# A delta-rule attention block and its SwiGLU block on one core: the third chunk moved to the seven-product scheme

## The chip, the cores and the metric

The kernel runs on one core of a Trainium2 chip. The metric is the device time in microseconds (us) of one execution, as the median of several runs. A core has five engines that each work through their own list of instructions in order: TensorE (PE, with its weight loads PEld) multiplies matrices into PSUM, VectorE (DVE) and ScalarE (ACT) do elementwise work, GpSimd (POOL) does small things, and SyncE (SP) issues the transfers (DMA). They wait for one another through semaphores.

## The reference

Two blocks follow each other. The first is a recurrence over 768 steps for 4 batches of 8 heads of width 48; the second multiplies its output, seen as 3072 tokens of width 384, through a gated layer of width 1536.

```python
k_n = k / (np.linalg.norm(k, axis=-1, keepdims=True) + 1e-06)
for t in range(S):
    kt, vt, bt = (k_n[:, :, t], v[:, :, t], beta[:, :, t, None])
    y[:, :, t] = np.einsum('bhd,bhde->bhe', q[:, :, t], state)
    v_old = np.einsum('bhde,bhd->bhe', state, kt)
    state = state + bt[:, :, :, None] * np.einsum('bhd,bhe->bhde', kt, vt - v_old)
...
x = np.ascontiguousarray(attn_out.transpose(0, 2, 1, 3)).reshape(B * S, H * D)
g = x @ w_gate
silu = g * (1.0 / (1.0 + np.exp(-g)))
val = x @ w_val
return (silu * val @ w_out).astype(np.float32)
```

All inputs and outputs are fp32.

## The kernel before

**Chunks.** The 768 steps are cut into 12 chunks of 64. A chunk has 256 tokens (4 batches), and its token matrix `xts[c]` holds 3 blocks of 128 features by 256 tokens. While TensorE works on the gated layer of chunk c, the recurrence of chunk c + 1 is fed in between in small steps. `advance(c)` does four: `p_r` and `p_y` (products with the state; VectorE subtracts p_r from v, the tile `vin`), `p_u` (with the inverted matrix Z), `p_s` and a second `p_y` (the new state), and `p_f` (turning the output into `xts[c]`, copied by ScalarE as x_ffn). `products` turns k and q of a later chunk and forms `p_g`. For each pair g of chunks a triangular matrix is inverted on VectorE: `invert(g)` runs `substitute`, 31 pairs of a product into `tmp` (L519) and a sum into `zb` (L525) that depend on each other; ahead of it GpSimd takes a root (`n_b`, L661) and sets a diagonal. Then ScalarE copies parts of Z, and a join (`p_j`) puts the halves together on TensorE.

**The order.** No scheduler decides it: the order in which the code issues instructions is the order on each engine. `point(c)` issues the next step of the recurrence of chunk c, or of its preparation. `fill(n)` issues VectorE's substitution steps for a budget n; `point_and_fill` does both and takes off the budget what the step itself gave VectorE (`spent`).

**The plain scheme (chunks 0 to 2).** `gate_val` (L1006) multiplies the 3 feature blocks with pieces of 128 gate and value columns, 256 tokens wide: 72 matmuls a chunk. `output` (L1035) makes 2 x 12 matmuls of 384 columns. An fp32 matmul leaves two records in the profile.

**The fast scheme (chunks 3 to 11, `FAST = 3`).** Products of two-by-two blocks are made with seven block products instead of eight, at the price of sums. In the gate/value part the blocks are halves of the tokens and pairs of weight columns (`f1`, `f2`) against the first two feature blocks; the third feature block is done plainly. A chunk has three rounds. `product4` (L922) is four matmuls of 128 tokens; a round has 11 of them where the plain scheme needs 12. `begin` is the first of a round, and its result is copied by ScalarE into a second PSUM bank to which further products are added. The four banks of a round are `p_x`, `p_w`, `p_y`, `p_v` (banks ffn_67 to ffn_70). VectorE forms sums of products in place (L1079), the gated hidden values `h` (L952), and sums of h for the output (`sums_of_h`). `output_fast` (L1122) makes seven products of six matmuls of 192 columns.

**The sums of weights.** The fast scheme needs sums of blocks of the weights. Those of gate and value (`sums_of_w`, 24 operations of 256 columns) are made on VectorE while chunk 2 runs; nine of them (`w_s`, three for each round) are stored in DRAM (`kept`), and each round loads the next round's three (`next_sums`, 256 KB each) into the same place. Those of the output weights (`combos`, four) are made by VectorE in the first two rounds of chunk 3. The sums of the tokens (`sums_of_x`, tile `x_t`) are made just before each fast chunk.

**Loads.** `load_v`, `load_k` and `load_blocks` (k and q, cut into rows of 32 steps) are issued on SyncE at the point where the tile they write becomes free.

Of the kernel before, what the change touches and what calls it, by code (L numbers as in the profile page):

```python
# [15 lines left out]
R = 32  # L16
# [4 lines left out]
def kernel(  # L21
# [304 lines left out]
    spent = []  # L326
# [85 lines left out]
    def turned(c, of_q, tag=None):  # L412
# [7 lines left out]
        if c >= blocks_of[of_q][1]:  # L420
            xt_v = xt.rearrange("p (bp b j i) -> p bp j b i", bp=NB, b=2, j=NJ)
            (qt if of_q else kt)[c] = xt_v
            blocks = blocks_of[of_q][2]
            nc.vector.transpose(xt, blocks.rearrange("p bp h d -> p (bp h d)"))
            spent.append(1.8)
            if c + 1 < NCH:
                load_blocks(of_q, c + 1)
            return
# [185 lines left out]
    def join_late(g, c, tags):  # L614
# [15 lines left out]
        t2 = work.tile([128, M, R], FP32, name="t2", tag="tmp", bufs=1)  # L630
# [19 lines left out]
    def invert(g):  # L650
# [16 lines left out]
        for _ in range(2 if g == 1 else 4):  # L667
            yield WAIT
# [25 lines left out]
        for s in range(2):  # L694
            hi = slice(64 * s, 64 * s + R)
            for c in range(2):
                z = ztp[g % ZB][hi, c]
                nc.scalar.copy(z[:, :, 0:R], z[:, :, R:C])
                yield 0.5
# [6 lines left out]
    def join(g):  # L706
# [14 lines left out]
        t2 = work.tile([128, 2, M, R], FP32, name="t2", tag="tmp", bufs=1)  # L721
# [19 lines left out]
    def advance(c):  # L741
# [45 lines left out]
        if c + 2 < NCH:  # L787
            load_v(c + 2)
# [14 lines left out]
        def of_state():  # L803
# [15 lines left out]
            for later in range(AHEAD, NCH):  # L819
                if rows_freed_by(later) == c:  # L820
                    load_k(later)
# [41 lines left out]
    def units(t):  # L863
        return t.rearrange("p (u n) -> p u n", u=4)

    w_s = {1: units(hp[6]), 2: units(hp[7]), 4: units(p_places[0][:, 0:512])}
    m5 = units(p_places[0][:, 512:1024])
    kept = {
        (n, r): dram.tile([128, 4, 128], FP32, name=f"w_s{n}_{r}")
        for n in w_s  # L870
# [8 lines left out]

    def sums_of_w(f):  # L880

        if f <= 4:
            r = (f // 2 + 1) % 3
            f1, f2 = 2 * r, 2 * r + 6
            for n in (1, 2, 4):
                for m in range(2):
                    s_ = w_s[n][:, 2 * m : 2 * m + 2]
                    if n == 1:
                        plus(s_, w_pair(m, 0, f2), w_pair(m, 1, f2))
                    elif n == 2:  # L890
                        minus(s_, w_s[1][:, 2 * m : 2 * m + 2], w_pair(m, 0, f1))
                    else:
                        minus(s_, w_pair(m, 1, f1), w_s[2][:, 2 * m : 2 * m + 2])
                nc.sync.dma_start(out=kept[n, r], in_=w_s[n])
        if f >= 6:
            for m in range(2):
                minus(w_pair(m, 0, f), w_pair(m, 0, f - 6), w_pair(m, 0, f))
# [32 lines left out]
    def summed_w(n):  # L930
        return lambda u: w_s[n][:, u]
# [4 lines left out]

    def gate_val_fast(c, r, fill):

        f1, f2 = 2 * r, 2 * r + 6
        x = xts[c]  # L940

        def next_sums(n):
            if c < NCH - 1 or r < ROUNDS - 1:
                nc.sync.dma_start(out=w_s[n], in_=kept[n, (r + 1) % ROUNDS])
# [14 lines left out]
        def combo_or_fill(n):  # L959
            if combos:  # L960
# [6 lines left out]
        product4(p_w, summed_w(1), x_t[:, 0], True)  # L967
        nc.scalar.copy(m5, p_w)
        next_sums(1)
        product4(p_y, summed_w(2), x_t[:, 1])  # L970
        nc.scalar.copy(p_v, p_y)  # L971
        next_sums(2)
        product4(p_x, plain(1, f1), x[:, 1, tok[0]])
# [7 lines left out]
        point_and_fill(c + 1, 3.4, combo_or_fill)  # L981
        product4(p_y, summed_w(4), x[:, 1, tok[1]])
        next_sums(4)
        product4(p_y, plain(2, f1), x[:, 2, tok[1]])
# [12 lines left out]
        point_and_fill(c + 1, 5, combo_or_fill)  # L997

    def gate_val(c, f, fill, within=None, behind=None):

        ps = {}
        for w_sb, name in ((wg_sb, "p_gate"), (wv_sb, "p_val")):
            ps[name] = ps_ffn([128, 2, TOK], name)
            for i in range(2):
                for t in range(KT):
# [4 lines left out]
                        start=(t == 0 and (i == 0 or c < 2)),  # L1010
# [8 lines left out]
        new_h(c, f, len(hs) if c < 2 else f // 2)  # L1019
        nc.vector.tensor_tensor(out=hs[c, f], in0=sil, in1=ps["p_val"], op=ALU.mult)  # L1020
        if c == FAST - 1 and 0 < f < 6:
            sums_of_w(f)
        if behind is not None:
            point(behind)
        if c == FAST - 1 and not 0 < f < 6:
            sums_of_w(f)
        fill(2 if c == FAST - 1 and f <= 6 else 3)

    def output(c, bp, fill, between=()):
        p_o = ps_ffn([128, DM], "p_o", bp if c == FAST - 1 else None)  # L1030
        for f in range(FT):
            if f in between:
                fill(2)
                point(2)
            nc.tensor.matmul(  # L1035
# [23 lines left out]
    FAST = 3  # L1059
# [49 lines left out]
    def output_fast(c, fill):  # L1109

        p = {}

        def clear(x, part):
            p[x, part] = ps_ffn([128, DH], "p_o", 2 * x + part)
            nc.scalar.copy(p[x, part], mask_q[:, 0:1].to_broadcast([128, DH]))
# [19 lines left out]
        clear(1, 0)  # L1135
        left, right = slice(0, DH), slice(DH, DM)
        product(0, 0, lambda f: h_of(c, f, 0), quarter(0, 0))
        nc.scalar.copy(o[0][:, right], p[0, 0])
        clear(1, 1)
        product(0, 1, lambda f: s_of(2, f), lambda f: w_t2[:, f])  # L1140
        plus(o[0][:, right], o[0][:, right], p[0, 1])
        fill(2)
        product(1, 0, lambda f: h_of(c, f, 1), lambda f: w_t3[:, f])
        plus(o[1][:, right], o[0][:, right], p[1, 0])
        fill(2)
        point(c + 1)
        product(0, 0, lambda f: h_of(c, f + FH, 0), quarter(1, 0))
        nc.scalar.copy(o[0][:, left], p[0, 0])
        for f in range(0, FH, 2):
            minus(h_of(c, f + FH, 0), h_of(c, f + FH, 0), s_of(2, f))  # L1150
        product(1, 1, lambda f: s_of(1, f), lambda f: w_t1[:, f])
        plus(o[1][:, right], o[1][:, right], p[1, 1])
        point(c + 1)
        product(
            1,
            0,
            lambda f: h_of(c, f + FH, 1),
# [323 lines left out]
```

## Time and profile before

| | before |
|---|---|
| median of 3 runs | 717.18 us (717.02 to 718.13) |
| the profiled execution | 716.87 us, span 715.2 us |
| granted TensorE clock, mean | 0.968 |
| TensorE busy | 681.8 us (95%) |
| VectorE busy | 463.9 us (65%) |
| ScalarE busy | 254.4 us (36%) |
| GpSimd busy | 51.7 us (7%) |
| moved by DMA | 60.19 MB, mean 84 GB/s |

The span is the time from the first to the last instruction in the trace; the device time has 1.67 us more around it. Busy times overlap each other. A line such as L922 is a line of the kernel before; "out<-in" names the tiles that an instruction writes and reads. Idle time is put down to the engine or transfer that ended it. In the changed kernel the same code stands some lines further down: L922 becomes L957, L1006 L1052, L1035 L1077, L1122 L1160, L1079 L1121, L952 L992.

### The profile page before, as it was taken

Reading aid. Unit: us, or ns where it says so; the run is one execution under the profiler, and the core shown is the slowest. Engines: PE = TensorE matmul, PEld = TensorE weight load, DVE = VectorE, ACT = ScalarE, POOL = GpSimd, SP = SyncE. Lnnn points to the kernel's source line nnn. Section 1 sums busy time; section 2 is a strip of 40 time slices with the busy share of each in tenths; the row PEclk is TensorE's granted clock in tenths of the full one; section 3 lists DMA queues with packets and bytes.
Section 4 is the critical chain, followed back from the end, with each engine's and each line's share of the span. In section 5 each row is a group of like instructions: output and inputs, shape, how many; then the busy total and the mean of one; then the engine's idle time right before and its main releaser. Section 6 shows DMA issues by size and latency. Waiting matters only on the chain.

```text
span 715.2 us, 25294 instructions
## 1 busy us (share of the span) xinstructions
PE 681.8 (95%) x11212; PEld 629.1 (88%) x11212; DVE 463.9 (65%) x1052; ACT 254.4 (36%) x536; POOL 51.7 (7%) x46
## 2 busy tenths in 40 slices
PE   4757999999999999999999999999999999999997
PEld 3546788866788799999999999999999999999997
DVE  6995765777499476688756789459864435333342
ACT  3467755302331342233333234232153033142230
POOL 8003000203000003000030000300000000000000
PEclk9656999999999999999999999999999999999999
DMA  7785443002343134344424444144142222121211
GB/s 149 172 232 171 123 118 127 23 12 47 72 113 76 27 71 115 61 102 117 69 82 105 59 95 99 30 97 109 35 112 70 46 75 60 49 65 45 67 45 23
DMA packets 143278, 60.19 MB, mean 84 GB/s; under 512 B 124256, under 2 KB 127328, under 8 KB 143168
## 3 DMA queue, kind: packets, MB, share of 16 engines
q1 hardware_dynamic: 140672, 58.00, 33.8%
q8 instruction: 88, 1.44, 0.8%
q10 hardware_dynamic: 2112, 0.39, 0.3%
q0 software_dynamic: 384, 0.17, 0.1%
q14 instruction: 22, 0.18, 0.1%
HBM read 51.46 MB, written 7.08 MB: 82 GB/s over the span
## 4 chain that ended last, share of the span: by engine, by line
PE 88%; DVE 5%; ACT 3%; issue 1%; POOL 1%; DMA 1%; SPq 0%; ACTq 0%; DVEq 0%
PE ffn L922 37%; PE ffn L1122 17%; PE ffn L1006 12%; PE ffn L1035 7%; PE p_g L447 3%; DVE tmp L519 2%; DVE zb L525 2%; PE p_u L775 2%; PE p_r L753 2%; PE p_s L806 2%; PE p_y L762 1%; PE p_y L794 1%; PE p_f L840 1%; POOL n_t L363 1%; PE p_j L639 1%
## 5 line engine op out<-in xcount | busy, mean ns | idle before, releaser
L922 PE MATMUL ffn<-x_ffn,wg_sb 128*128 128x128 f32 x756 | 115.4, 275 | 0.3 <-DVE ffn L1079 0.3
L922 PE MATMUL ffn<-x_ffn,wv_sb 128*128 128x128 f32 x756 | 115.3, 275 | 0.0
L922 PEld LDWEIGHTS ffn<-x_ffn,wg_sb 128*128 128x128 f32 x756 | 100.1, 192 | 0.7 <-DVE ffn L1079 0.5
L922 PEld LDWEIGHTS ffn<-x_ffn,wv_sb 128*128 128x128 f32 x756 | 99.6, 192 | 0.0
L947 ACT ACTIVATE sil<-ffn 128x256 f32<-128x256 f32 x108 | 41.4, 383 | 122.0 <-PE ffn L922 120.1
L952 DVE TENSOR_TENSOR h_f<-sil,ffn 128x256 f32<-128x256 f32 x108 | 44.6, 418 | 48.5 <-ACT sil L947 46.6
L1122 PE MATMUL ffn<-wo_sb,h_f 128*128 128x192 f32 x432 | 75.2, 327 | 0.0
L1122 PEld LDWEIGHTS ffn<-wo_sb,h_f 128*128 128x128 f32 x432 | 70.3, 190 | 0.3
L1079 DVE TENSOR_TENSOR ffn<-ffn,p_sb 128x512 f32<-128x512 f32 x54 | 37.6, 697 | 50.0 <-ACT ffn L971 48.8
L525 DVE TENSOR_TENSOR zb<-zb,tmp 128x31 f32<-128x31 f32 (+15 forms) x186 | 63.7, 343 | 6.4
L519 DVE TENSOR_TENSOR tmp<-zb,mb 128x31 f32<-128x31 f32 (+15 forms) x186 | 63.3, 340 | 5.1
L922 PE MATMUL ffn<-x_t,h_f 128*128 128x128 f32 x432 | 54.9, 280 | 0.0
L1006 PE MATMUL ffn<-x_ffn,wg_sb 128*128 128x256 f32 x216 | 52.4, 393 | 1.2 <-ACT x_ffn L843 1.2
L922 PEld LDWEIGHTS ffn<-x_t,h_f 128*128 128x128 f32 x432 | 50.6, 191 | 1.1
L1006 PE MATMUL ffn<-x_ffn,wv_sb 128*128 128x256 f32 x216 | 49.9, 380 | 0.0
L661 POOL TENSOR_TENSOR n_b<-mb,half 128x32 f32<-128x32 f32 x5 | 28.0, 5591 | 300.5 <-DVE mb L489 261.0
L1079 DVE TENSOR_TENSOR o_sb<-o_sb,ffn 128x192 f32<-128x192 f32 x45 | 15.8, 351 | 51.3 <-PE ffn L1122 48.4
L1006 PEld LDWEIGHTS ffn<-x_ffn,wg_sb 128*128 128x128 f32 x216 | 41.2, 196 | 7.5 <-ACT x_ffn L843 1.7
L1035 PE MATMUL ffn<-wo_sb,h_f 128*128 128x384 f32 x136 | 45.7, 490 | 0.0
L1006 PEld LDWEIGHTS ffn<-x_ffn,wv_sb 128*128 128x128 f32 x216 | 40.7, 190 | 5.5
L1035 PEld LDWEIGHTS ffn<-wo_sb,h_f 128*128 128x128 f32 x136 | 25.3, 190 | 16.5
L935 ACT COPY ffn<-ffn 128x512 f32<-128x512 f32 x27 | 15.4, 570 | 55.9 <-PE ffn L922 55.9
(229 smaller groups left out, 1038.7 us busy)
## 6 DMA issues: line engine op xcount, KB each, us to landing
h_f<-w_s SPq DMA_DIRECT2D x52, 256.0 KB
p_sb<-w_s SPq DMA_DIRECT2D x26, 256.0 KB
vin<-in_v_dram SPq DMA_DIRECT2D x96, 48.0 KB
out_dram<-o_sb SPq DMA_DIRECT2D x48, 96.0 KB
kn<-in_k_dram SPq DMA_DIRECT2D x40, 96.0 KB
zt<-in_moe_w_out_dram SPq DMA_DIRECT2D x6, 384.0 KB
qpad<-in_q_dram SPq DMA_DIRECT2D x36, 64.0 KB
wo_sb<-in_moe_w_gate_dram SPq DMA_DIRECT2D x4, 512.0 KB
```

The costliest lines, as they stand in the source:

```text
L447: nc.tensor.matmul(p_v[par][half_of(b if of_q else b ^ par), bp, j], kt[c][half_of(par), bp, j, b], xt[half_of(par), bp, j, b],)
L519: nc.vector.tensor_tensor(out=t_v, in0=zb[:, 0 : j + 1, j : j + 1].to_broadcast([128, j + 1, m]), in1=mb[:, j : j + 1, j + 1 : R].to_broad ...
L525: nc.vector.tensor_tensor(out=zb[:, 0 : j + 1, j + 1 : R], in0=zb[:, 0 : j + 1, j + 1 : R], in1=t_v, op=ALU.add,)
L661: nc.gpsimd.tensor_tensor(out=n, in0=mb.rearrange("p j i -> p (j i)")[:, 0 : R * R : R + 1], in1=half, op=ALU.pow,)
L922: nc.tensor.matmul(p[:, u], w(u), moving, start=start and u == 0, stop=True, skip_group_check=True,)
L935: nc.scalar.copy(p_y, p_x)
L947: nc.scalar.activation(sil[:, n].rearrange("p (i n) -> p i n", i=2), p[:, 0:2], ACTF.Silu)
L952: nc.vector.tensor_tensor(out=h_of(c, f, j), in0=sil[:, n].rearrange("p (i n) -> p i n", i=2), in1=p[:, 2:4], op=ALU.mult,)
L1006: nc.tensor.matmul(ps[name][:, i], w_sb[:, t, (f + i) * 128 : (f + i + 1) * 128], xts[c][:, t], start=(t == 0 and (i == 0 or c < 2)), stop ...
L1035: nc.tensor.matmul(p_o, hs[c, f - f % 2][:, f % 2, bp * 128 : (bp + 1) * 128], wo_sb[:, f], start=(f == 0), stop=(f == FT - 1),)
L1079: nc.vector.tensor_tensor(out=out, in0=a, in1=b, op=ALU.add)
L1122: nc.tensor.matmul(p[x, part], a(f - f % 2)[:, f % 2], b(f), start=not begun and f == 0, stop=f == FH - 1, skip_group_check=True,)
```

## The change

`FAST` becomes 2: chunk 2 is computed by the fast scheme, like chunks 3 to 11. With it come these edits.

- The 24 sums of weights move ahead of chunk 2, into the last output of chunk 1 (12 operations before the v subtraction, 8 between it and the state sum, 4 behind the token sums of chunk 2). They lie in h tiles that are free at that time (`made_in`). Chunk 2 reads its first round's sums in place and reloads the later ones; its first `m5` lies in hp[13].
- `sums_of_x(2)` runs before chunk 2, and `begin(2, 0)` behind the step of the recurrence that is issued there, which is the first half of a join.
- The four combos move into the rounds and the output of chunk 2.
- The output of chunk 2 takes its seven products in an order of its own, and forms the differences of h behind `product_4`. The two PSUM areas to which outputs are added are cleared on ScalarE: the first in the last gate/value round, of every fast chunk, the second in the output.
- The temporary `t2` of the joins lies in the ring "r" of two tiles instead of in the substitution's `tmp`.
- The copies of Z on ScalarE are spread over more filling (budget 2 each, 1 for g = 2, instead of 0.5).
- From chunk 2 on `load_v`, `load_k` and `load_blocks` go into a list, `late_loads`, and are issued one at a time behind the second and the third reload of weight sums of a round.
- The fill budgets of chunk 2 and of the first round of chunk 3 are 1.5 larger.

```diff
+    def load_late():
+        if late_loads:
+            late_loads.pop(0)()
...
             if c + 1 < NCH:
-                load_blocks(of_q, c + 1)
+                late_loads.append(lambda: load_blocks(of_q, c + 1))
...
-        t2 = work.tile([128, 2, M, R], FP32, name="t2", tag="tmp", bufs=1)
+        t2 = work.tile([128, 2, M, R], FP32, name="t2", tag="r", bufs=2)
...
-        for _ in range(2 if g == 1 else 4):
+        for _ in range({1: 2, 2: 3}.get(g, 4)):
...
-                yield 0.5
+                yield 1 if g == 2 else 2
...
+    made_in = {
+        0: {1: hp[6], 2: hp[7], 4: hp[10]},
+        1: {1: hp[1], 2: hp[2], 4: hp[0]},
+        2: {1: hp[12], 2: hp[13], 4: hp[8]},
+    }
...
+    sums_at = {
+        2: [(1, 1), (2, 1), (4, 1)],
+        4: [(1, 2), (2, 2), (4, 2)],
+        6: [(3, 1), (3, 2)],
+        8: [(1, 0), (2, 0)],
+        12: [(4, 0), (3, 0)],
+    }
...
+    def clear(part):
+        area = ffn_banks[2 + part][:, 0:DH]
+        nc.scalar.copy(area, mask_q[:, 0:1].to_broadcast([128, DH]))
...
+        more = 1.5 if (c, r) <= (FAST + 1, 0) else 0
+
+        def combo_and_fill(n):
+            if c == FAST:
                 combos.pop(0)()
                 n -= 1.9
             fill(n)
...
         next_sums(2)
+        load_late()
...
-        point_and_fill(c + 1, 3.4, combo_or_fill)
-        product4(p_y, summed_w(4), x[:, 1, tok[1]])
+        point_and_fill(c + 1, 3.4 + more, fill)
+        product4(p_y, summed_w(4, c), x[:, 1, tok[1]])
         next_sums(4)
+        load_late()
...
         if r < ROUNDS - 1:
             begin(c, r + 1)
-        point_and_fill(c + 1, 5, combo_or_fill)
+        else:
+            clear(0)
+        point_and_fill(c + 1, 5 + more, combo_and_fill)
...
-    FAST = 3
+    FAST = 2
...
+        else:
+            clear(1)
+            first_product()
+            product_5()
+            nc.scalar.copy(o[1][:, right], p[1, 1])
+            product_4()
+            combos.pop(0)()
+            differences()
+            fill(1)
+            point(c + 1)
+            product_2()
+            plus(o[1][:, right], o[1][:, right], o[0][:, right])
+            nc.scalar.copy(o[1][:, left], o[0][:, right])
+            fill(1)
+            product_3()
+            plus(o[1][:, right], o[1][:, right], p[1, 0])
+            point(c + 1)
+            product_7()
+            store(c, 0, o[0])
+            x_sums(c + 1)
+            product_6()
+            plus(o[1][:, left], o[1][:, left], p[1, 0])
+            store(c, 1, o[1])
         fill(5)
...
         finish(2)
+        x_sums(2)
+        sums_of_w(12)
         for c in range(2, NCH):
-            if c >= FAST:
+            if c > FAST:
                 begin(c, 0)
             point(c + 1)
-            if c >= FAST:
-                for r in range(ROUNDS):
-                    gate_val_fast(c, r, fill)
-                output_fast(c, fill)
-            else:
-                for f in range(0, FT, 2):
-                    gate_val(c, f, fill, behind=c + 1)
-                output(c, 0, fill)
-                point(c + 1)
-                output(c, 1, fill)
+            if c == FAST:
+                begin(c, 0)
+            for r in range(ROUNDS):
+                gate_val_fast(c, r, fill)
+            output_fast(c, fill)
             finish(c + 1)
             x_sums(c + 1)
```

## The prediction

> **What bounds the kernel now.** I read the page first: busy times, then the chain that ended last. TensorE is busy for 95% of the span and holds 88% of the chain.
>
> ```profile
> PE 681.8 (95%) x11212; PEld 629.1 (88%) x11212; DVE 463.9 (65%) x1052; ACT 254.4 (36%) x536; POOL 51.7 (7%) x46
> ```
>
> A busy share proves little by itself, so the chain in order of time comes next: start, length, line, number of matmul records (an fp32 matmul leaves two).
>
> ```profile
> 187.98 5.45 PE ffn L1006 x24
> 193.43 1.93 PE p_j L639 x95
> 195.36 10.56 PE ffn L1006 x48
> ...
> 229.18 7.94 PE ffn L1035 x24
> ...
> 245.51 0.89 PE ffn L922 x8
> ...
> 354.97 0.89 PE ffn L922 x8
> ...
> 409.48 0.89 PE ffn L922 x8
> ...
> 667.77 29.58 PE ffn L922 x264
> 697.35 13.67 PE ffn L1122 x84
> ```
>
> Chunk 2 (plain, L1006 and L1035) holds TensorE from 187.98 to 245.51, 57.53 us. Chunk 5 (fast, L922 and L1122) takes 409.48 - 354.97 = 54.51. The last two lines are the last chunk, with no recurrence in it: bare, a fast chunk is 29.58 + 13.67 = 43.25 us. TensorE's own waits between 187 and 345 us are two:
>
> ```profile
> PE ffn L922 <- DVE ffn L1079: 0.3, 1, 0.3
> PE ffn L1006 <- ACT x_ffn L843: 0.2, 1, 0.2
> ```
>
> So TensorE bounds by its work and other engines only by fractions of a us. How full is VectorE beside it? Chunks 2 to 5, one row each (columns: length, then busy us of PE, PEld, DVE, ACT, POOL, granted clock, DMA share, GB/s):
>
> ```profile
> 187.98:245.51 57.53, 57.53 (x776) 45.73 (x777) 44.14 (x112) 14.13 (x26) 0.00 (x0) 1.00 0.31 73
> 245.51:300.51 55.00, 55.00 (x1061) 53.76 (x1060) 34.71 (x62) 20.22 (x42) 6.58 (x3) 1.00 0.36 80
> 300.51:354.97 54.46, 54.18 (x933) 53.09 (x932) 45.93 (x115) 21.19 (x46) 0.00 (x0) 1.00 0.49 95
> 354.97:409.48 54.51, 54.51 (x1060) 53.37 (x1060) 36.72 (x84) 18.14 (x38) 6.58 (x3) 1.00 0.38 82
> ```
>
> VectorE is busy 44.1 of 57.5 us in chunk 2; the clock is full. Its real pace is seen in the order of time (start, length): independent operations start before the one ahead has ended, 0.335 us apart at 256 columns though each lasts 0.42; the dependent pair of the substitution does not overlap.
>
> ```profile
> 210.39 0.42 DVE L1079 TENSOR_TENSOR h_f<-wg_sb 128x256 f32<-128x256 f32 x1
> 210.73 0.42 DVE L1079 TENSOR_TENSOR h_f<-wv_sb 128x256 f32<-128x256 f32 x1
> ...
> 216.32 0.42 DVE L519 TENSOR_TENSOR tmp<-zb,mb 128x256 f32<-128x256 f32 x1
> 216.78 0.42 DVE L525 TENSOR_TENSOR zb<-zb,tmp 128x256 f32<-128x256 f32 x1
> ```
>
> **TensorE's work.** Chunk 2 plain: L1006 is 5.45 + 10.56 + 3 x 5.38 = 32.15 us for 144 records, L1035 7.94 + 7.74 = 15.68, together 47.83. Fast: chunk 5 less its recurrence (p_j 2 x 1.22, p_r, p_y, p_u, p_s, p_y, p_f 5.76, p_g 2.02) is 54.51 - 10.22 = 44.29, which is the bare 43.25 plus about 0.15 at each of seven joints between kinds of matmul. Chunk 2 keeps one p_j of 1.93, the 5.76 and the 2.02 and has six joints: 53.9 us against 57.53, a gain of 3.6.
>
> [...] The row: a 128-column record takes 29.58/264 = 0.112 us, a 256-column one 5.18/24 = 0.216, so halving the width halves the time, though twice the weights are loaded per column. [...] I take the row: it is this kernel, in fp32.
>
> **The start of chunk 2.** `begin(2, 0)` waits for x_ffn, at 187.94 as now. The next product wants x_t[0]. VectorE: the state sum (183.78) is followed by 0.88, the n_b group 1.52, mb 1.14, a first substitution pair 0.45 and vin 0.86, so x_t[0] ends at 188.95, and begin at 188.9: 0.1 lost. ScalarE's copy p_y<-p_x stands behind d_o and t (187.95 to 189.64 now) and ends at 190.2; the summed product that needs it could start at 189.9: 0.35 lost. Both are new waits: +0.45.
>
> **VectorE, the disputed part.** The 24 sums of weights (0.335 each, 8.0 us) leave chunk 2 for 170.6 to 191. Before the vin subtraction at 177.54 stand now 12 of them: transposes to 170.6, six sums 2.0, mb 2.1, six 2.0, vin 0.86, end 177.55; the 4 us idle ahead of that row hides them. Eight more fall between it and the state sum (2.7 into 5.3 us of idle). GpSimd's n_b pow starts 2 us later (about 175 to 181, then its memset to 182), and VectorE wants it at 184.7: hidden. The last four run beside begin, needed by p_v at 193. If this cover were gone each sum would cost TensorE 0.335.
>
> Inside chunk 2 VectorE then has, start to start: x_t and last sums 2.3; three rounds of 2 x 0.60 (L1079), 4 x 0.36 (h), 1.1 (sums of h), 3.8 each, 11.4; the substitution from its second pair on 22.9; transposes of k and q twice 4.7; masks 1.2; vin, state, vin 2.6; the four combos 1.3 + 1.25 + 1.3 + 1.34, brought from chunk 3, 5.2; differences 1.0; o_sb 1.6; x_t of chunk 3 0.8. That is 53.7; adding what it must wait for in round 0 (0.9 for ScalarE's p_v copy, then 0.2), it comes free of the x_t of chunk 3 at about 243.3. TensorE would reach that chunk's begin at 242.4 and, after its p_g of 2.0, want x_t at 245.4. Slack 2 us. The gates on the way, VectorE ready against TensorE needing: round 1's p_y sum 206.5/208, round 2's 219.9/221.2, sums of h ahead of `product_5` 227.9/229.8 (behind ScalarE's second clearing, 229.8 too), t2 230.5/234.4, differences 235.8/238.2, the o_sb sum that frees the bank of `product_6` 239.8/240.2. All are met, by 0.4 to 4 us, so I book nothing.
>
> [...] The rows' lengths agree (0.42), their starts do not (0.335). Paid in full by some 50 independent operations, 0.085 each, VectorE would need 58 us, overrun the slack by 2, and leave a gain of under 2. I take the starts.
>
> **Waits, queues and order.** SyncE: the nine stores of sums move from 194.9-216.4 to behind the 16 block loads, whose issue ends at 182.5; at the 360 GB/s that a burst of three showed here (0.96 share at 203 to 204), eight take 6 us, to about 190. Behind the fifth stands ScalarE's m5 copy into hp[13] at 190.3, behind the third the h of round 0 at 193.5. The v load (6.1 us of issue) now follows the second reload of round 0 and holds up the third to 197.6, needed at 208. Nine more reloads, 0.7 us each, run in a stage of 0.35 to 0.5 DMA share: nothing, unless the stores land 2 us late, and then 1 us for each. The late k, q and v loads are wanted a chunk (54 us) after: nothing. t2 in "r" takes away the substitution's wait for the join's second product; with "tmp" it would have held VectorE to 195.4. `clear(0)` waits for round 2's second h (226.5), ahead of y (227.9); 0.33 of ScalarE, nothing. Z copies spread: chunk 3's p_y copy had stood behind three of them (1.75 us to 247.6), now it has none ahead.
>
> **Chunks 3 and 4.** Chunk 3 took 55.0, and chunk 5 with the same pieces 54.5. Chunk 4 (54.46) holds 43.25 + 5.76 + two p_g 4.04 and joints 0.9, 53.9; there the chain runs through VectorE from 328.9 to 336.1, substitution in front of the sums TensorE wants. Up to 1.0 is there to regain. The third inverse now begins in chunk 3, where the combos made room, but it can stand in the way elsewhere: between 0.5 lost and 1.0 gained, I take 0.6 gained, near what chunk 5 shows. From chunk 5 on the pieces are the same: 0.
>
> **Sum**: -3.6 + 0.45 - 0.6 = -3.8. The profiled execution took 716.87 (span 715.2 and 1.67 around it), so 713.1; the median of the runs stands 0.3 above it: **713.4 us**.
>
> **Rivals.**
> - VectorE is late by parts (waits that I booked at nothing, ScalarE between): 1.5 to 3.5 us of stalls in chunk 2's last round and its outputs. For it: 54 us of work in 54. Against it: every gate has slack. Gain 0.3 to 2.3: 715 to 717. Chance 0.17.
> - VectorE becomes the bound outright, at one place: its in-order queue from round 2 to the x_t of chunk 3. Each us above 56 (54 and the slack of 2) is a us of TensorE; from 59.8 us on the 3.8 are gone. With full lengths (58) and a tenth of a us for each wait on some 30 operations it is 61, giving 718.5. Chance 0.12.
> - The spreading also takes stalls from later chunks, 0.1 to 0.2 in each of eight: 711.5 to 712.3. Against: those chunks show no wait of TensorE. Chance 0.09.
> - [...] Chunk 5 speaks against it: 0.02, in the slower share.
>
> **How the numbers follow.** My forecast, 712.4 to 714.6, has 0.60. The range 711.9 to 716.2 takes in most of the first and third rival. A measurement of this kernel tells about 0.2%, 1.4 us: faster is below 715.75, which the forecast, the third rival and over half of the first give, 0.80; same 0.07; slower 0.13.
>
> **What would show it.** Right: from chunk 2's begin to chunk 3's about 54.3 us, with 264 + 84 narrow records; VectorE busy above 90% there and TensorE's waits for it under 1 us; chunks 3 and 4 near 54.6 and 54. Wrong: waits of TensorE for L1121, L1145 or L992 of more than 1.5 us between 219 and 246, a wait of m5 for a store, or the x_t of chunk 3 after its p_g.

## The result: 715.0 us, and the profile after

The changed kernel took 714.99 us (median of 7 runs, 713.93 to 715.73) beside 717.11 us for the kernel before (7 runs, 716.67 to 718.39). The ratio is 0.9964, with a 95% interval of 0.9953 to 0.9976: faster by 2.1 us, 0.4%. Measured again (e8 below) it took 714.38 us beside 718.18, 3.8 us less, with a ratio of 0.9949 [0.9933, 0.9964]. Its profiled execution took 713.96 us with a span of 712.3 us, 2.9 us less than the profiled execution before (716.87 and 715.2). The forecast was 713.4 us. The median lies inside the range on record (711.9 to 716.2), but just above the narrower forecast of 712.4 to 714.6.

First the page after, busy times of the engines. TensorE has more records (the narrow scheme) and less time; VectorE has gained the sums.

```profile
PE 679.6 (95%) x11368; PEld 637.9 (90%) x11368; DVE 475.6 (67%) x1085; ACT 261.8 (37%) x555; POOL 53.8 (8%) x46
```

Then its chain in order of time (start, length, engine, tile, line, records), with the start of chunk 2, of chunks 3 to 6, and the last chunk.

```profile
189.26 0.21 DVE x_t L1118
...
189.50 0.30 DVE x_t L1118
189.81 0.38 ACT t L638
190.19 0.50 ACT ffn L970
...
190.74 3.84 PE ffn L957 x32
...
228.58 6.05 PE ffn L1160 x36
...
235.28 7.80 PE ffn L1160 x48
243.08 0.89 PE ffn L957 x8
...
297.60 0.89 PE ffn L957 x8
...
351.51 0.89 PE ffn L957 x8
...
406.24 0.89 PE ffn L957 x8
...
664.94 29.57 PE ffn L957 x264
694.52 13.67 PE ffn L1160 x84
```

Chunk 2 starts on TensorE at 188.52 and ends at 243.08. Both new waits at its start are here: the x_t made after vin, and ScalarE's `t` and then its copy into the second bank (L970), which release TensorE at 190.74. After that TensorE runs to chunk 3 without a break. The last chunk, bare of recurrence, still takes 43.24 us.

The same stretches as before, one row each (length, then busy us of PE, PEld, DVE, ACT, POOL, granted clock, DMA share, GB/s), chunks 2 to 5:

```profile
188.50:243.08 54.58, 54.50 (x932) 53.39 (x933) 50.62 (x120) 21.15 (x45) 0.00 (x0) 1.00 0.42 93
243.08:297.60 54.52, 54.52 (x1061) 53.46 (x1060) 40.05 (x91) 20.27 (x42) 6.58 (x3) 1.00 0.35 75
297.60:351.51 53.91, 53.91 (x932) 53.01 (x932) 40.62 (x95) 21.42 (x46) 0.00 (x0) 1.00 0.50 99
351.51:406.24 54.73, 54.73 (x1060) 53.51 (x1060) 38.18 (x88) 18.13 (x38) 6.58 (x3) 1.00 0.34 75
```

VectorE is busy 50.62 of 54.58 us in chunk 2, 93%, and behind the start of the chunk TensorE does not wait for it. In the list of TensorE's waits from 183 to 352 us one line is left; before the change there was also one of 0.3 us for a sum in place (L1079):

```profile
PE ffn L957 <- ACT x_ffn L856: 0.2, 1, 0.2
```

Where the 2.9 us between the two profiled executions come from, by chunk. "To chunk 3" runs from `p_r` in the last output of chunk 1 to the start of chunk 3, so that it holds the moved sums and the new waits too.

| stretch | before | before, second profile (e10) | changed | changed, second profile (e8) |
|---|---|---|---|---|
| start of the kernel to `p_r` | 176.40 | 176.98 | 176.89 | 177.13 |
| `p_r` to chunk 3 | 69.11 | 69.51 | 66.19 | 66.20 |
| chunk 3 | 55.00 | 55.91 | 54.52 | 54.51 |
| chunk 4 | 54.46 | 54.46 | 53.91 | 53.91 |
| chunk 5 | 54.51 | 54.70 | 54.73 | 54.70 |
| chunk 6 | 54.56 | 54.55 | 54.55 | 54.55 |
| chunk 7 | 50.79 | 50.79 | 50.79 | 50.79 |
| chunk 8 | 53.58 | 53.58 | 54.00 | 54.05 |
| chunks 9 and 10 | 99.36 | 99.36 | 99.36 | 99.36 |

Between the first profiles: +0.49 - 2.92 - 0.48 - 0.55 + 0.22 + 0.42 = -2.8, and the spans differ by 2.9. The rest of this document asks which of these terms belong to the change.

### The profile page after: what moved, and what is told of

Read it like the earlier page. It is cut to its first block, busy times and chain, and to the rows that moved or that the text cites. A ratio compares the mean times of both kernels' runs of the same rounds, so it can differ in the third digit from the quotient of the medians.

```text
span 712.3 us, 25668 instructions
## 1 busy us (share of the span) xinstructions
PE 679.6 (95%) x11368; PEld 637.9 (90%) x11368; DVE 475.6 (67%) x1085; ACT 261.8 (37%) x555; POOL 53.8 (8%) x46
## 3 DMA queue, kind: packets, MB, share of 16 engines
q8 instruction: 89, 1.46, 0.8%
## 4 chain that ended last, share of the span: by engine, by line
PE 89%; DVE 5%; ACT 3%; issue 1%; DMA 1%; SPq 0%; DVEq 0%; ACTq 0%
PE ffn L957 42%; PE ffn L1160 19%; PE ffn L1052 9%; PE ffn L1077 4%; PE p_g L452 3%; PE p_s L816 2%; PE p_r L760 2%; PE p_u L782 2%; DVE tmp L524 2%; DVE zb L530 2%; PE p_y L769 1%; PE p_y L804 1%; PE p_f L853 1%; DMA kn<-in_k_dram 1%; PE p_j L723 1%
## 5 line engine op out<-in xcount | busy, mean ns | idle before, releaser
L957 PE MATMUL ffn<-x_ffn,wg_sb 128*128 128x128 f32 x840 | 128.3, 275 | 0.4 <-ACT x_ffn L856 0.2
L957 PE MATMUL ffn<-x_ffn,wv_sb 128*128 128x128 f32 x840 | 128.1, 275 | 0.0
L1160 PE MATMUL ffn<-wo_sb,h_f 128*128 128x192 f32 x480 | 83.4, 327 | 0.0
L992 DVE TENSOR_TENSOR h_f<-sil,ffn 128x256 f32<-128x256 f32 x120 | 49.6, 418 | 47.6 <-ACT sil L987 45.1
L1160 PEld LDWEIGHTS ffn<-wo_sb,h_f 128*128 128x128 f32 x480 | 78.1, 190 | 0.4
L957 PE MATMUL ffn<-x_t,h_f 128*128 128x128 f32 x480 | 61.2, 280 | 0.1
L957 PEld LDWEIGHTS ffn<-x_t,h_f 128*128 128x128 f32 x480 | 56.2, 191 | 1.4 <-ACT ffn L970 0.3
L970 ACT COPY ffn<-ffn 128x512 f32<-128x512 f32 x30 | 17.1, 571 | 63.6 <-PE ffn L957 57.2
L1052 PE MATMUL ffn<-x_ffn,wg_sb 128*128 128x256 f32 x144 | 35.8, 401 | 0.9 <-ACT x_ffn L856 0.9
L1160 PE MATMUL ffn<-last_k,h_f 128*128 128x192 f32 x200 | 35.9, 327 | 0.0
L1052 PE MATMUL ffn<-x_ffn,wv_sb 128*128 128x256 f32 x144 | 33.4, 381 | 0.0
L1160 PEld LDWEIGHTS ffn<-last_k,h_f 128*128 128x128 f32 x200 | 32.9, 190 | 0.0
```

What stands on the lines that cost most here:

```text
L957: nc.tensor.matmul(p[:, u], w(u), moving, start=start and u == 0, stop=True, skip_group_check=True,)
L970: nc.scalar.copy(p_y, p_x)
L992: nc.vector.tensor_tensor(out=h_of(c, f, j), in0=sil[:, n].rearrange("p (i n) -> p i n", i=2), in1=p[:, 2:4], op=ALU.mult,)
L1052: nc.tensor.matmul(ps[name][:, i], w_sb[:, t, (f + i) * 128 : (f + i + 1) * 128], xts[c][:, t], start=(t == 0 and i == 0), stop=(t == KT - 1),
L1160: nc.tensor.matmul(p[x, part], a(f - f % 2)[:, f % 2], b(f), start=not begun and f == 0, stop=f == FH - 1, skip_group_check=True,)
```

## Experiments

The theory at the start: chunk 2 gains by TensorE's own work; two small waits at its start and the spread of Z's copies in chunk 8 give some of it back; VectorE has room, but not much. The main rival: VectorE or a transfer already limits chunk 2, so that part of the gain was lost there unseen. All kernels are the changed kernel with one edit, unless said otherwise.

**e1: Z's copies together again for g = 5.**

```diff
-                yield 1 if g == 2 else 2
+                yield 1 if g == 2 else 0.5 if g == 5 else 2
```

> The changed kernel, with the copies of Z of the sixth pair (g = 5) alone back at a budget of 0.5; only ScalarE's order around chunk 8 changes. Theory (the spread copies cost 0.4 us in chunk 8, where two of them stand between the y copies and ScalarE's copies of p_w and p_y): chunk 8 falls from 54.0 to 53.6 us, every other chunk stays within 0.05 us, 0.4 us less in all. Rival (the 0.4 us is a difference between executions or comes with the late loads): chunk 8 stays at 54.0.

Measured 714.04 us (713.23 to 714.25), ratio 0.9952 [0.9937, 0.9967]. Chunk 8 took 53.59 us, as before the change. In the changed kernel the chain of chunk 8 had left TensorE:

```profile
527.79 2.00 PE ffn L957 x16
...
529.81 0.12 ACT zt L705
...
529.94 0.61 ACT zt L705
...
530.58 0.58 ACT p_sb L1010
531.17 0.50 ACT ffn L1013
...
531.71 1.16 PE ffn L957 x8
```

Two spread copies of Z (L705) stand ahead of L1010 and L1013 on ScalarE, and TensorE needs L1013. In e1 TensorE ran through the same place, as the chain of e1 shows:

```profile
528.34 4.66 PE ffn L957 x40
```

So the 0.42 us in chunk 8 belong to the spreading, and are regained without it. The other chunks were as in the changed kernel, but for chunk 4, 54.18 (+0.27): there the small products `p_y` took 1.21 us instead of 0.93, at the place where e2 and e7 stop (see e12).

**e2: the d_o copies early.** ScalarE's two copies into d_o, which stand ahead of `t` at the start of chunk 2, are issued inside chunk 1's last output, ahead of its h block 6 (the join then takes these copies).

```diff
                 if (c, bp) == (1, 1):
                     sums_of_w(f)
+                    if f == 6:
+                        early_d[1, 1] = odd_half(1, 1)
...
```

> The changed kernel, with ScalarE's two copies d_o of the second join of g = 1 issued before the p_u copies instead of behind x_ffn. Theory (at the start of chunk 2 TensorE waits 0.45 us: 0.1 for x_t, 0.35 for the copy of p_x to p_y that stands behind d_o and t): chunk 2 becomes 0.3 to 0.4 us shorter, the rest stays. Rival (the wait is for x_t, behind the inverse on VectorE): under 0.1 us.

Measured 714.17 us (713.78 to 715.1), ratio 0.9958 [0.9943, 0.9972]. `p_r` to chunk 3 took 65.88 us, 0.31 less: ScalarE's queue at the start of chunk 2 was a cost of about the forecast size (0.35). But the span was 713.4 us, because chunk 4 took 55.14 us instead of 53.91. Its chain there:

```profile
305.10 1.08 PE p_r L771 x64
306.17 0.69 PE p_y L780 x45
306.86 0.93 issue
307.79 0.55 PE p_y L780 x19
```

"Issue" is time in which TensorE waited for nothing that the profile shows, in the middle of a group of small products. It was not in the theory; e7, e9 and e12 show what it is.

**e3: t2 in the substitution's `tmp`.**

```diff
-        t2 = work.tile([128, 2, M, R], FP32, name="t2", tag="r", bufs=2)
+        t2 = work.tile([128, 2, M, R], FP32, name="t2", tag="tmp", bufs=1)
```

(and the same in the join of g = 1, `join_late`.)

> The changed kernel, with t2 of every join back in the substitution's tmp. Theory: the substitution's second pair in chunk 2 must wait for the join's second product, about 3 us later than now, and stands in front of the sums that TensorE wants; VectorE's slack there is 1 to 2 us, so TensorE loses 1 to 2 us in chunk 2. Rival (the tag is of no weight, VectorE catches up in the waits that it has anyway): under 0.3 us.

Measured 716.21 us (715.46 to 718.27), ratio 0.9988 [0.9979, 0.9998]: most of the gain is gone. `p_r` to chunk 3 took 67.81 us, 1.62 more. The substitution's next product into `tmp` stood idle for 3.30 us, until the join's second product (L646) had read t2 (VectorE in order of time). From there the chain runs through VectorE: the substitution stands ahead of the h blocks (L992), and TensorE waits for these until 203.68 (end of the chain).

```profile
196.77 0.22 DVE L524 TENSOR_TENSOR tmp<-zb,mb 128x60 f32<-128x60 f32 x1 [3.30 <-PE p_j L646]
```

```profile
202.88 0.75 DVE h_f L992 x2
...
203.68 4.73 PE ffn L957 x40
```

One small edit of the change, the other buffer for t2, carries over half of what chunk 2 brings.

**e4: the loads of k, q and v at once** instead of behind the reloads of the weight sums.

```diff
-                late_loads.append(lambda: load_blocks(of_q, c + 1))
+                load_blocks(of_q, c + 1)
...
-                late_loads.append(lambda: load_v(c + 2))
+                load_v(c + 2)
```

(and the same for `load_k`; `load_late` does nothing.)

> The changed kernel, with the loads of v, k and the k and q blocks issued at once from chunk 2 on, as before, instead of behind the reloads of sums. Theory (SyncE's queue is hidden either way; the reloads are wanted some 10 us after they are issued): within 0.2 us of the changed kernel in every chunk. Rival (eight issues of 0.6 us ahead of a reload make the product wait): 0.3 to 1 us lost in chunk 2 or in each of the chunks 3 to 8.

Measured 714.88 us (714.38 to 715.88), ratio 0.9967 [0.9954, 0.998], not to be told from the changed kernel by its runs. In the profile `p_r` to chunk 3 took 66.59 us, 0.40 more: about 0.13 at the start of chunk 2, and 0.27 between 198.18 and 208.50. There TensorE stops at 204.58 for the second of the weight sums of round 1. Its reload, held up on SyncE by the eight loads of v and stores behind them, was issued at 201.37 and landed at 204.55; in the changed kernel it was issued at 192.37 and landed at 195.68, 7 us before it was wanted. So the rival had the wait right, a little under the smallest size that it gave, and in this profile the deferring brings about 0.3 us. Chunks 3 to 10 were the same.

**e5 and e6: more work for VectorE.** Four, and nine, idle sums of 512 columns (0.70 us each) at the end of round 1 of chunk 2.

```diff
+        if (c, r) == (FAST, 1):
+            idle = p_places[0][:, 0:512]
+            for _ in range(4):
+                plus(idle, hs[c, 0].rearrange("p i n -> p (i n)"), hs[c, 0].rearrange("p i n -> p (i n)"))
```

> The changed kernel with four more VectorE sums of 512 columns (about 2.6 us) at the end of chunk 2's second round; they write a place that nothing reads. Theory (VectorE is just short of being the bound in chunk 2; its sum of p_y in the third round is ready 1.2 us before TensorE wants it): TensorE loses 2.6 - 1.2 = 1.4 us in chunk 2. Rival (it has slack of 2 us and more, as the gate at chunk 3 suggests): 0 to 0.6 us.

> The same with nine more sums (about 5.7 us). Theory (a slack of 1.2 us, then us for us): 4.5 us lost in chunk 2, so that the whole is slower than the kernel before. Rival (slack of 2 us or waits further on that take up more): 3.5 us or less.

e5: 715.98 us (one run), `p_r` to chunk 3 67.64, 1.45 more for four sums that held VectorE for 2.86 us. The theory (2.6 - 1.2 = 1.4) met the number, but three things go into it. VectorE had been idle for 0.5 us ahead of `vin` in the changed kernel, and the sums fill that first. The sum in place of round 2 then ends at 223.48 instead of 220.76, 2.15 us later when the later `p_r` (0.57) is taken off, and TensorE, which wanted it at 221.90 in the changed kernel, waits 1.1 us:

```profile
PE ffn L957 <- DVE ffn L1125: 1.1, 1, 1.1
```

So the room at this gate, where the prediction had 1.3 (219.9 against 221.2), is 1.1 us. The last 0.3 us go at a second gate, `product_6`, which starts at 242.89, as soon as the o_sb sum ahead of it has ended at 242.84.

e6: 721.42 us (one run), `p_r` to chunk 3 72.85, 6.66 more. TensorE's waits in chunk 2 of e6:

```profile
PE ffn L957 <- DVE ffn L1125: 3.4, 1, 3.4
PE p_u L782 <- DVE vin L777: 1.3, 1, 1.3
```

They are 4.7 us, near the theory's 4.5. Without the clock's part below, e6 lost 3.3 us more than e5 for 3.6 us more of VectorE's work: past the room, each us of VectorE cost TensorE about 0.9 here. The other 1.9 us are the clock: rows of e6 by us (length, PE busy, granted clock, DMA share, GB/s) at the end of the wait:

```profile
224.00:225.00 1.00, 0.02 (x4) 0.75 0.07 27
225.00:226.00 1.00, 0.00 (x0) 0.50 0.24 49
...
230.00:231.00 1.00, 1.00 (x7) 0.50 0.33 51
231.00:232.00 1.00, 1.00 (x9) 0.84 0.00 0
```

The granted clock fell to half during the wait and came back some 4 us after TensorE had work again; the 40 records from 227.38 took 6.60 us instead of 4.66. So nine sums cost more than us for us.

**e7: `begin(2, 0)` ahead of the step of the recurrence** instead of behind it.

```diff
-            if c > FAST:
-                begin(c, 0)
+            begin(c, 0)
             point(c + 1)
-            if c == FAST:
-                begin(c, 0)
```

> The changed kernel, with begin(2, 0) ahead of the step of the recurrence (the first half of the join), as in the chunks after it. Theory (the join's first half is free where it stands, in TensorE's wait for x_ffn): it then costs its 0.7 us and saves the 0.35 us wait for ScalarE's copy, 0.2 to 0.4 us lost. Rival (the copy behind d_o is what counts): 0.3 us gained.

Measured 715.07 us (714.66 to 715.5), ratio 0.9955 [0.9938, 0.9972]. `p_r` to chunk 3 took 66.65 us, 0.46 more: TensorE stands 0.9 us for x_ffn, a time in which the first half of the join (L634) ran in the changed kernel. Chunk 4 took 55.14 again, with a stop of 0.92 us after the 45th record of `p_y`: the same instruction as in e2, in a kernel with another edit.

**e8: the changed kernel again.**

> The changed kernel itself, unchanged, for a second profile. Theory (the 0.5 us by which its first profile is behind the kernel before at 171 us, where nothing is changed, is a difference between executions): another offset at 171 us, and the same chunk lengths to 0.1 us. Rival (something in the changed program costs it): 0.5 us again.

714.38 us (713.84 to 715.33), ratio 0.9949 [0.9933, 0.9964]. The chunks repeat to 0.05 us (last column of the table), with no stop in chunk 4.

**e9: both repairs**, the early d_o of e2, and Z's copies spread for g = 2 alone (0.5 for all later groups).

```diff
-                yield 1 if g == 2 else 2
+                yield 1 if g == 2 else 0.5
```

> The changed kernel with two repairs: ScalarE's d_o copies of chunk 2 issued before the chunk begins (as in e2), and Z's copies spread for g = 2 alone, the later groups with the budget of 0.5 that they had in the kernel before. Theory (the two losses are independent, and chunk 5's 0.22 us is the spread of Z's copies too, as chunk 8's 0.42 was): from p_r to chunk 3's start 65.9 us, chunk 5 at 54.5, chunk 8 at 53.6, and the sum 0.3 + 0.2 + 0.4 = 0.9 us below the changed kernel, about 714.0 us against its 714.7 to 715.0; if TensorE's stop of 0.9 us with nothing waited for appears in chunk 4 again (55.1 instead of 53.9), nearly all of that is eaten. Rival: the spread relieves chunks 3 and 4, and putting the copies together again costs there what chunk 8 regains (chunk 4 rose by 0.27 in e1): no gain over the changed kernel.

Measured 716.15 us (714.43 to 716.66, 11 runs), ratio 0.9976 [0.9967, 0.9985]: slower than the changed kernel, against the theory and for another reason than the rival's. `p_r` to chunk 3 was 66.00. The budgets decide which step of the recurrence lands where, and with the shorter ones the small products of two joins (L734, L748) moved on TensorE, from chunk 5 into chunk 4 and in chunk 6 from the output into the rounds. Chunk 6 took 55.50 (54.55 in the changed kernel) and chunk 8 55.20. There is no wait for another engine there; the chain of e9 in chunk 8:

```profile
550.76 1.05 PE p_j L748 x72
551.81 0.96 issue
552.78 0.37 PE p_j L748 x19
```

**e10: the kernel before, profiled again.**

> The kernel before, profiled a second time, to tell the 0.5 us by which the changed kernel reaches the end of chunk 1 later. If it is variation of the start-up, p_r of output (1,1) comes anywhere from 176.4 to 178.4 us, as it did in the profiles of the changed kernels; if it belongs to the change, it comes at 176.4 again. Chunk lengths should repeat to 0.1 us: 57.5, 55.0, 54.5, 54.5, 54.6, 50.8, 53.6, 50.8, 48.6.

It ran 718.91 us (one run, span 717.2). `p_r` came at 176.98, 0.58 later than in the first profile and later than the changed kernel's 176.89. So nothing shows that the +0.49 at the start belongs to the change; it is there already at 171 us (170.81 against 171.29 for the first half of the join), ahead of the moved work. The changed kernels came to `p_r` between 176.70 and 178.41, mostly later than both profiles of before, so two profiles do not exclude a small share either. Chunk 5 took 54.70 here, and 54.70 to 54.73 in the profiles of the changed kernel: its +0.22 is not shown to belong to the change. The 0.40 us in `p_r` to chunk 3 lie in the output's records behind the first `p_y` (L1035), at the place of e11's loss below. Chunk 3 took 55.91, because TensorE stood 1.1 us for a reload of weight sums, which the first profile did not have:

```profile
PE ffn L922 <- DMA h_f<-w_s: 1.1, 1, 1.1
```

In the chain the reload, which lands 3.41 us after 271.90, stands behind 16 loads of k and q on SyncE (L169, 261.94 to 271.80). That is the order which `late_loads` takes away. In the first profile the same reload was issued at 270.48 and came in time.

**e11: both repairs without moving anything on TensorE**: the early d_o with e1's copies for g = 5 alone.

> The changed kernel with the two repairs that worked singly: the d_o copies early (e2) and Z's copies put together for g = 5 alone (e1), so that no group of head-join transposes moves in TensorE's order as it did in e9. Theory (the sizes of e1 and e2 add up, and e9 lost because TensorE stopped with nothing waited for in two groups of transposes that had moved): p_r to chunk 3's start 65.9 us, chunk 8 at 53.6, no stop in chunks 6 and 8 (54.55 and 50.8 for 6 and 7), and chunk 4 at 54.2, or 55.1 if the stop seen there in e2 and e7 comes again; about 713.7 to 714.3 us, or 714.6 to 715.2 with the stop. Rival (the two repairs disturb each other, e9's loss is theirs): no faster than e1's and e2's 714.0 to 714.2, and stops in chunks 6 and 8 again.

Measured 713.75 us (712.91 to 714.25), ratio 0.9942 [0.9929, 0.9955], the fastest median of all. Chunk 8 took 53.73, chunks 6 and 7 54.55 and 50.79, chunk 4 53.93 without the stop. `p_r` to chunk 3 was 66.21 instead of 65.9: 0.3 us were lost in the last output of chunk 1, two pairs of records taking 0.84 and 0.91 us where four in a row take 1.49, with 0.05 of "issue" between them (a stop like e2's, see e12); from x_ffn to chunk 3 it is as in e2 (54.25 and 54.24). The interval overlaps that of the changed kernel, so its lead over it is likely, not shown.

**e12: the same kernel, TensorE's instructions shifted by 128.**

```diff
-            nc.tensor.matmul(p_v[hi, par, 1, h], k_v[:, 0], k_v[:, 0])
+            for _ in range(2 if h < 4 else 1):
+                nc.tensor.matmul(p_v[hi, par, 1, h], k_v[:, 0], k_v[:, 0])
```

> The same kernel with 32 of the first small matmuls on the keys issued twice (the same value into the same place), while TensorE waits for its first data: 128 more instructions on TensorE (each matmul shows as two matmul and two weight-load records), half of one of the 16 KB packets in which TensorE's instructions are fetched (89 packets of 1.46 MB in all for 22,736 records of 64 bytes). It costs 32 x 2 x 0.03 = 1 to 2 us of the start at most. Theory (a stop with nothing waited for is TensorE out of instructions at the end of a packet): the stop of chunk 4, after the 45th of the 64 records of p_y, goes away or comes 64 records earlier, inside p_r, and stops may appear in other groups of transposes, those of the head join and p_u, p_s. Rival (the stop belongs to the burst of loads at that time, or to the transposes themselves): the stop stays where e2 and e7 had it, after the 45th record of p_y.

Measured 717.94 us (716.43 to 720.33, 12 runs), ratio 1.0007 [0.9996, 1.0017]: 4.2 us above e11, for 32 tiny matmuls. They cost nothing where they stand (`p_r` came at 177.41, in e11 at 177.44). TensorE's waits in e12 from 80 us on:

```profile
PE p_j L749 <- issue: 0.6, 1, 0.6
PE ffn L1174 <- issue: 0.5, 1, 0.5
PE p_j L658 <- issue: 0.3, 1, 0.3
PE ffn L969 <- issue: 0.2, 1, 0.2
PE p_y L816 <- issue: 0.2, 1, 0.2
PE ffn L969 <- ACT x_ffn L868: 0.2, 1, 0.2
PE p_u L794 <- issue: 0.2, 1, 0.2
```

In e11 only the wait for x_ffn is in that list. Six stops have come, all in or shortly behind groups of small products. Against e11 the profile lost 1.08 us up to chunk 3, 0.80 in chunk 3, 0.49 in chunk 5 and 0.54 in chunk 6 (chunk 8 gained 0.14), together 2.8, the difference of the spans; the medians are further apart (4.2), and of the other executions there is no profile. The expectation itself was not tested at its place: e11, which e12 has to be held against, has no stop in `p_y` of chunk 4 either. The trace lists transfers of instructions, too. The queue whose packets fit TensorE's records in number, in the kernel before, the changed kernel and e12 (packets, MB, share):

```profile
q8 instruction: 88, 1.44, 0.8%
```

```profile
q8 instruction: 89, 1.46, 0.8%
```

```profile
q8 instruction: 90, 1.47, 0.8%
```

1.46 MB in 89 packets is 16 KB a packet (16,384 bytes each in the traces of before and after). TensorE's records, matmuls, weight loads and some 150 semaphore waits, are 22,575, 22,895 and 23,023, which is 88.2, 89.4 and 89.9 times 256, within one of the packets. So one packet goes with 256 records, a block, and the places of the stops can be tried against the blocks. Number all of TensorE's records in the trace from 0 in order of start. The stops without a named wait, with the record that comes late, the time at which the transfer of the last packet before it ended, and the time at which TensorE goes on:

| run | record | in | packet landed | TensorE goes on |
|---|---|---|---|---|
| e2 | 10433 | `p_y` of chunk 4 | 306.35 | 307.78 |
| e7 | 10433 | `p_y` of chunk 4 | 306.66 | 308.16 |
| e8 | 5825 | join of g = 1, first half | 187.39 | 188.88 |
| e9 | 15553 | join, chunk 6 | 444.56 | 445.97 |
| e9 | 18881 | L968, chunk 8 | 547.14 | 548.48 |
| e9 | 19137 | join, chunk 8 | 551.44 | 552.78 |
| e11 | 5313 | L1090, output of chunk 1 | 179.03 | 180.53 |
| e12 | 5569, 5825 | `p_u`, `p_y` of chunk 2's recurrence | 181.02, 184.90 | 182.33, 186.33 |
| e12 | 6337 | join, chunk 2 | 196.47 | 197.89 |
| e12 | 8897 | join, chunk 3 | 263.98 | 265.28 |
| e12 | 12481 | L969, chunk 5 | 361.66 | 363.08 |
| e12 | 16065 | L1174, chunk 6 | 458.70 | 460.05 |

Each of these numbers is 193 more than a multiple of 256, and each time TensorE goes on 1.3 to 1.5 us after the packet landed. The stop of e8 cost nothing, because TensorE had to wait for x_ffn anyway. The small losses of e1 (chunk 4) and e10 are at records 10433 and 5313 too. In all 14 profiles no block begins sooner than 1.24 us after its packet landed. So these numbers fit TensorE waiting for its next block of instructions, and the rivals (the burst of loads alone, the small products alone) are out: they cannot pick out one record in 256.

In the first profiles of before and after no block from 54 us on is late: its first record comes at most 0.22 us after the record ahead of it, which is one matmul record of 256 columns. A block lasts long among large matmuls, where some 18 records, weight loads included, pass in a us (0.112 us for a matmul record of 128 columns, so 256 records take some 14 us), and not in a group of small ones, where 64 matmuls and 64 weight loads pass in 0.93 to 1.08 us. `p_r` and `p_y` together are 256 records in 2.0 us, while the transfer of a packet took 0.88 to 1.78 us in the changed kernel (median 0.97), and its block began 1.3 us after that or later. In e2 the packet for record 10433 was moved from 305.12 on, 7.6 us into chunk 4; in the changed kernel from 303.87 on, 6.3 us into it, and there the record came 1.86 us after the landing, unhindered. What makes a packet start a us later in one execution than in another, these runs do not show.

## Why the prediction was right

Taken by its own steps:

- **TensorE's work in chunk 2, forecast 53.9 us, and the new waits, 0.45.** Chunk 2 took 188.52 to 243.08 = 54.56 us, where 54.35 was the sum; from `p_r` on the gain is 2.92 us (3.3 against the second profile of before, which lost 0.4 there, see e10) where 3.15 was booked. The matmul work repeats the rows it was taken from (6.05 and 7.80 for the output, 29.57 and 13.67 in the bare chunk). 264 narrow records took 29.57 us again, 0.112 us each, against 0.216 for a record of 256 columns in the kernel before: half the width took half the time. So the rival with the chance of 0.02, that the narrow scheme doesn't save in chunk 2, is out.
- **x_t late by 0.1, ScalarE's copy by 0.35.** x_t ended at 189.47 with `begin` ending at 189.41; moving d_o out of ScalarE's way returned 0.31 (e2). Both about as booked.
- **VectorE has 2 us of room.** Right in kind: no wait for it in the profile behind the start. Its order was followed closely, with a start 0.49 us later than in the profile that the forecast times come from. VectorE in order of time, after:

```profile
220.07 0.69 DVE L1121 TENSOR_TENSOR ffn<-ffn,p_sb 128x512 f32<-128x512 f32 x1
...
235.08 1.09 DVE L1118 TENSOR_TENSOR h_f<-h_f,h_f 128x256 f32<-128x256 f32 x3
...
239.75 0.34 DVE L1121 TENSOR_TENSOR o_sb<-o_sb,ffn 128x192 f32<-128x192 f32 x1
```

  The sum in place of round 2 ends at 220.76 (forecast 219.9, TensorE wants it at 221.90, forecast 221.2). The differences end at 236.17 (forecast 235.8), the o_sb sum at 240.09 (forecast 239.8, `product_6` starts at 240.97, forecast 240.2), and the last x_t of chunk 3 at 243.53 (forecast 243.3). Three operations in 1.09 us are the pace of 0.335 from start to start. By starts, not by full lengths, was the right reading: some 50 operations at 0.085 more (0.42 of length less 0.335 from start to start) would have been 4 us, which the 1.1 us at round 2 and the 0.9 at `product_6` do not hold. The room that decides is not the 2 us of the last gate but the 1.1 us at round 2 (e5), where the list of gates had 1.3. So the 2 us were the wrong number to carry into the rival: work put at the end of round 1 costs TensorE time from about 1.6 us on (0.5 of idle and 1.1 of room), not from 2.
- **t2 in "r".** Booked as what keeps VectorE from 195.4; taking it away cost 1.62 us (e3).
- **Chunks 3 and 4, forecast -0.6.** They gave 0.48 + 0.55 = 1.03, the upper end of what the prediction had as possible. Against the second profile of before, chunk 3 gave 1.4, with the late reload in it. No experiment takes this gain apart; the wait of 0.3 us for a sum in place in chunk 4 is gone, the rest is not attributed.
- **From chunk 5 on: 0.** This is the term of the sum that was mis-sized. Chunk 8 lost 0.42, by the spread copies of Z ahead of L1010 and L1013 on ScalarE. The prediction had looked at chunk 3's copy alone, which the spreading helps, and not at later groups. The 0.22 of chunk 5 are in the second profile of before too (e10).
- **The start-up** was taken as equal. It differs by 0.6 us between the two profiles of before, and by up to 1.7 among those of the changed kernels.

So -3.8 was the forecast for the profiled execution, and -2.9 came. -2.92 up to chunk 3, -1.03 behind it and +0.42 in chunk 8 are -3.5, which the experiments and the repeated profiles leave to the change; +0.49 and +0.22 are not shown to belong to it. That the sum comes so near -3.8 is in part luck: 0.4 more in chunks 3 and 4 make up for the 0.42 of chunk 8, which was booked at nothing.

The median of the first measurement fell only 2.1 us, to 714.99, where the first rival (VectorE late by parts, 715 to 717) begins. It is not that rival: TensorE has no wait for VectorE from round 0 to chunk 3, and e5 had to add 2.9 us of work to make one. VectorE as the bound outright is excluded by the same for the kernel as it is. The gain of spreading in later chunks has the opposite sign in the one that was tried, chunk 8. That the median is 1 us above the profiled execution was not foreseen: the seven runs lie at 713.9 to 714.1 (three) and 715.0 to 715.7 (four). A gap of about 0.9 us is what one stop in chunk 4 costs. That such stops make the two groups is possible but not shown: neither profile of the changed kernel has one there.

## What to carry to other kernels

The scheme with fewer multiplications paid on a matmul-bound stage (2.92 us from `p_r` to chunk 3) because the engine that makes its sums still had room there, and that room is read gate by gate along its in-order queue: the smallest gate counted (1.1 us at round 2, e5), not the 2 us read at the last one. Spread helper work only where the engine it lands on has no short deadline: what relieves one chunk can stand ahead of a needed copy in another (0.42 us in chunk 8, e1). Where TensorE ran long groups of very small products, the time depended on where the blocks of instructions begin (2.0 us of stops in e9, 2.8 between the profiles of e11 and e12), so compare chunk lengths of several profiles before a small gain or loss is put down to an edit.

## What the runs showed of the hardware that was not expected

- TensorE's instructions came in packets of 16 KB, one for 256 records (89 packets for 22,895 records in the changed kernel), and no block began sooner than 1.24 us after its packet had landed. TensorE stopped for 0.2 to 1.0 us and went on 1.3 to 1.5 us behind the landing of a packet, always at the same record of 256, inside or shortly behind groups of small products (e2, e7, e8, e9, e11, e12). 128 records more at the start moved the blocks and cost 4.2 us of the median, none of it where they stood (e11 and e12).
- The granted clock of TensorE fell to half from about 224.5 us on, half a us into a wait of 3.4 us that followed one of 1.3 us, and stayed there until about 231.3, some 4 us after work had come (e6). Between the two waits lay about 1.1 us of work, `p_u`. The lower clock cost 1.9 us beyond the wait itself: 40 records took 6.60 us instead of 4.66.
- Without any edit the start-up of the kernel before varies by 0.6 us between two executions, and a reload of 256 KB that stands behind 16 other loads on SyncE came in time in one and cost 1.1 us in the other (e10).
